# The first 512 tokens of an MLP in two halves, an attention's block means ahead of the weight loads, and a third weight matrix in the token tiles

## The chip, the cores and the metric

The kernel runs on one core of a Trainium2 chip. The metric is the time of one execution on the device in microseconds (us); the verdict compares medians of several executions. Engines are named as in the profile: PE (TensorE matmul), PEld (its weight loads), DVE (VectorE), ACT (ScalarE), POOL (GpSimd), SP (the engine that issues nearly all loads here).

## The reference

Attention over 2 batches, 8 heads, 768 positions and 64 dimensions, in which each query sees its neighbours within 16 positions and one summary per block of 32 (the maximum of the keys, the mean of the values). Its output, as 1536 tokens of 512 numbers, goes through two MLPs:

```python
def _attn_ref(q, k, v):
    k_sum = k.reshape(B, H, nb, block, D).max(axis=3)
    v_sum = v.reshape(B, H, nb, block, D).mean(axis=3)
    scores_l = np.where(mask_l, scale * q @ k.T, -1e9)          # |i - j| < 16
    scores_s = scale * einsum('bhsd,bhnd->bhsn', q, k_sum) + np.log(block)
    a = softmax(concatenate([scores_l, scores_s]))
    return a @ concatenate([v, v_sum])

x = attention as (1536, 512)
h = x @ w_in;  x = (h * sigmoid(1.702 * h)) @ w_out             # d_ff 2048, "layer 1"
x = (sigmoid(x @ w_gate) * (x @ w_val)) @ w_out2                # d_ff 1536, "layer 2"
```

The weights come in 64 bit floats.

## The kernel before

**Attention in 24 units.** A unit is one batch `b`, one group `g` of 256 query positions and one pair of heads `hp`; four units (all `hp`) make 256 tokens complete. A loop over `t` runs the parts of several units in one iteration (the list `ORDER`): scaled key windows `kx` on POOL (`w_copy`), scores `ps_s` on PE (`b_pe`: a mask matmul, then 4 of 128 columns), the row maximum `nm` on DVE, the exponential `e` on ACT (`b_exp`), the normalization on POOL, then for the unit three before it the transposes `ps_p`, their copy `pt`, the product with the value windows `ps_x` (`d_pe`), and the split of the result into two float32r tiles, `xH` on ACT and `xL` on DVE. `ps_s` has three PSUM buffers, so the mask matmul of unit u waits until the exponentials of unit u-3 are done.

**The means of the values** come from `vt`: `sum_load` brings it, `sum_v` reduces it on DVE (`vm`), `sum_lay` lays it out by PE and ACT (`ps_v`, `vs`), and `put_v` writes `vs` by DMA into the value windows `vwin`, which `d_pe` reads.

**Weights.** `fetch` loads one matrix of a group of 256 hidden columns twice, as `raw` and as a copy shifted by two bytes, `mid` (1 MB each); `load_group` decodes the pair on DVE and ACT (L104 to L119) into two float32r tiles, and each decode issues the next `fetch`. `raw` and `mid` have one buffer each; the second matrix (`1_0_1`) goes into free buffers of the token tiles `xH` and `xL`.

**MLP steps.** A step is (layer, group, block of 512 tokens). `first` makes 24 matmuls of 512 columns into `ps_h`, and the gating on ACT, DVE, ACT, POOL (`sg`, `gh`, `gl`); `second` makes 24 more into `ps_o` and adds them into `acc`. The first `EARLY` = 4 steps (blocks 0 and 1, groups 0 and 1) are put between the units of the attention by `filler`: one yield per iteration of `t`, two from t = 8, and no step before its tokens are complete (t = 10 for block 0, t = 18 for block 1). The exponential and the sigmoid use different tables of ACT, so a table is loaded at every change. The other steps follow the attention, with more PSUM buffers.

**What sets the order.** A scheduler places the instructions of PE, DVE, ACT and POOL; SP keeps the order in which the program is written. So a load that waits for a tile holds up all loads written behind it.

Of the kernel before, what the change touches and what calls it, by code (L numbers as in the profile page):

```python
# [8 lines left out]
F32 = mybir.dt.float32  # L9
F32R = mybir.dt.float32r  # L10
# [19 lines left out]
def attention_moe_moe2_kernel(ctx: ExitStack, tc: tile.TileContext, ins: dict, out: bass.AP):  # L30
    nc = tc.nc
# [92 lines left out]
    groups = [(1, g) for g in range(n1)] + [(2, g) for g in range(n2)]  # L124
    steps = [(1, g, blk) for blk in range(NTB) for g in range(2)]
    steps += [(layer, g, blk) for layer, g in groups[2:] for blk in range(NTB)]
    ends = {1: n1 - 1, 2: n2 - 1}
# [55 lines left out]

    def project(wh, wl, f, blk, name):
        ps = ps_h.tile([P, TB], F32, tag="h", name=name)
        c = slice(f * P, (f + 1) * P)
        mm3(ps, [((wh[:, kk, c], wl[:, kk, c]), (xH[blk][:, kk, :], xL[blk][:, kk, :])) for kk in range(KC)])
        return ps

    def first(layer, g, blk, batch=False):  # L190
        w = weights[layer, g]
        gh = gh_slots.tile([P, GF, TB], F32R, f"gh{layer}_{g}_{blk}")
        gl = gl_slots.tile([P, GF, TB], F32R, f"gl{layer}_{g}_{blk}")
        gt[layer, g, blk] = gh, gl

        def sigmoid(layer, ps):
            sg = sg_slots.tile([P, TB], F32, "sg")
            nc.scalar.activation(sg, ps, AF.Sigmoid, scale=1.702 if layer == 1 else 1.0)  # L198
            return sg

        def gated(f, ps, sg):
            nc.vector.tensor_tensor(out=sg, in0=ps, in1=sg, op=ALU.mult)  # L202
            nc.scalar.copy(gh[:, f, :], sg)  # L203
            nc.gpsimd.tensor_tensor(out=gl[:, f, :], in0=sg, in1=gh[:, f, :], op=ALU.subtract)  # L204

        if batch:
            held = []
            for f in range(GF):
                held.append(project(w[0], w[1], f, blk, "ps_h"))
                yield  # L210
            held = [(ps, sigmoid(layer, ps)) for ps in held]
            yield
            for f, (ps, sg) in enumerate(held):
                gated(f, ps, sg)
            yield
            return
        for f in range(GF):
            ps = project(w[0], w[1], f, blk, "ps_h")
            sg = sigmoid(layer, ps)
            if layer == 2:  # L220
                ps = project(w[2], w[3], f, blk, "ps_v")
            gated(f, ps, sg)
            yield

    def second(layer, g, blk, last, lag=False):
        w = weights[layer, g]
        wh, wl = w[-2], w[-1]
        gh, gl = gt.pop((layer, g, blk))
        if g == 0:
            acc[layer, blk] = (acc_a if blk < 2 else acc_b).tile([P, 4, 512], F32, tag=f"acc{blk}", name=f"acc{layer}_{blk}")  # L230
# [4 lines left out]
        for m in range(4):  # L235
            ps = ps_o.tile([P, 512], F32, tag=o_tag, name="ps_o")
            c = slice(m * P, (m + 1) * P)
            if layer == 1:
                mm3(ps, [((wh[:, f, c], wl[:, f, c]), (gh[:, f, :], gl[:, f, :])) for f in range(GF)])
            elif last and blk == NTB - 1 and m == 3:  # L240
# [14 lines left out]
            if g == 0:  # L255
                nc.scalar.copy(a[:, m, :], ps)
                if not lag:
                    yield
                continue
            nc.vector.tensor_tensor(out=a[:, m, :], in0=ps, in1=a[:, m, :], op=ALU.add)  # L260
            if last and layer == 1:
# [8 lines left out]
    acc_b = None  # L270
    EARLY = 4
    coming = (x for n in range(2) for x in load_group(*groups[n]))
# [10 lines left out]
    with tc.manual_schedule(engines={mybir.EngineType.SP}), ExitStack() as es:  # L283
# [225 lines left out]
        def filler():  # L509
            for layer, g, blk in steps[:EARLY]:  # L510
# [50 lines left out]
    with tc.manual_schedule(engines={mybir.EngineType.SP}):  # L561
# [66 lines left out]
```

## Time and profile before

| | |
|---|---|
| median of 3 executions | 665.69 us (665.18 to 666.26) |
| the profiled execution | 663.71 us, of which the span from first to last instruction is 661.9 |
| PE busy | 631.7 us, 95% of the span, 3168 matmuls |
| DVE, ACT, POOL busy | 415.2, 243.1, 187.2 us |
| mean granted clock of PE | 0.982 |
| moved by DMA | 93.97 MB, 142 GB/s over the span |

The span is to be read in two parts. From about 146 us to the end PE is busy without a gap, and nothing but the number and the width of its matmuls counts. Before that the attention runs with the first MLP steps between its units, and PE has gaps and stretches at half clock. The rows below show this first part.

### The profile page before, as it was taken

To read this page: it belongs to the slowest core of one execution; us is meant where nothing else is said; L and a number is where in the kernel's file an instruction comes from. 1 tells how busy PE (TensorE), PEld (TensorE's weight loads), DVE (VectorE), ACT (ScalarE), POOL (GpSimd) and SP (SyncE) were. 2 spreads that over 40 slices of the span, in tenths; PEclk is the share of its full clock that TensorE was granted. 3 is DMA by queue.
4 is the path that set the end of the run, shared out by engine and by line. 5 is a ranking of instruction groups with operands and counts; after the bars stand their busy time and mean duration, and the time that the engine had idled before them with its cause. 6 is when DMAs were issued, how large, how long until landed. Compare 5 with 4: busy or idle time off the path is not lost.

```text
span 661.9 us, 8251 instructions
## 1 busy us (share of the span) xinstructions
PE 631.7 (95%) x3168; PEld 515.1 (78%) x3170; DVE 415.2 (63%) x604; ACT 243.1 (37%) x498; POOL 187.2 (28%) x164
## 2 busy tenths in 40 slices
PE   6478799999999999999999999999999999999997
PEld 3255688778888888888888888888888888888886
DVE  6899656559998777777778626437627627422223
ACT  3355574746443333333345425313213213211110
POOL 6574576413332222213131112111111111211110
PEclk9778899999999999999999999999999999999999
DMA  9999773007775242434333034423414413000013
GB/s 314 351 372 325 223 236 94 3 13 276 255 261 198 93 171 99 159 111 145 118 138 111 20 124 143 147 92 140 176 66 151 182 49 128 0 1 0 13 67 112
DMA packets 39672, 93.97 MB, mean 142 GB/s; under 512 B 2128, under 2 KB 12624, under 8 KB 39632
## 3 DMA queue, kind: packets, MB, share of 16 engines
q1 hardware_dynamic: 39056, 92.39, 40.3%
q10 hardware_dynamic: 576, 1.05, 0.4%
q8 instruction: 25, 0.41, 0.2%
q14 instruction: 15, 0.12, 0.1%
HBM read 88.71 MB, written 3.15 MB: 139 GB/s over the span
## 4 chain that ended last, share of the span: by engine, by line
PE 88%; DVE 3%; DMA 3%; ACT 3%; POOL 1%; issue 1%; SPq 0%; DVEq 0%; ACTq 0%; POOLq 0%
PE ps_o L181 35%; PE ps_h L181 34%; PE ps_v L181 15%; DMA mid<-in_moe_w_in 2%; PE ps_s L381 2%; PE ps_x L429 1%; PE ps_p L414 1%; ACT e L394 1%; DMA vt<-in_vt 1%; DVE nm L386 1%; POOL kx L370 0%; ACT L198 0%; ACT L394 0%; DVE dc L110 0%; DVE dc L112 0%
## 5 line engine op out<-in xcount | busy, mean ns | idle before, releaser
L204 POOL TENSOR_TENSOR gl<-sg,gh 128x512 fp32r<-128x512 f32 x84 | 116.1, 1383 | 419.4 <-ACT gh L203 419.3
L260 DVE TENSOR_TENSOR acc<-ps_o,acc 128x512 f32<-128x512 f32 x143 | 96.3, 684 | 37.2 <-PE ps_o L181 36.8
L203 ACT CAST gh<-sg 128x512 fp32r<-128x512 f32 x84 | 52.1, 621 | 134.9 <-DVE sg L202 134.9
L198 ACT ACTIVATE sg<-ps_h 128x512 f32<-128x512 f32 x84 | 49.8, 596 | 139.2 <-PE ps_h L181 139.1
L202 DVE TENSOR_TENSOR sg<-ps_v,sg 128x512 f32<-128x512 f32 x36 | 24.8, 690 | 110.5 <-PE ps_v L181 110.0
L181 PE MATMUL ps_o<-gl,w_1H 128*128 128x512 f32 x192 | 75.6, 394 | 0.7 <-POOL gl L204 0.7
L181 PE MATMUL ps_o<-gh,w_1L 128*128 128x512 f32 x192 | 75.6, 400 | 0.5 <-ACT gh L203 0.4
L181 PE MATMUL ps_h<-xL,w_0H 128*128 128x512 f32 x192 | 75.7, 394 | 0.0
L181 PE MATMUL ps_h<-xH,w_0L 128*128 128x512 f32 x192 | 75.3, 396 | 0.0
L181 PE MATMUL ps_h<-xH,w_0H 128*128 128x512 f32 x192 | 75.3, 392 | 0.0
L181 PE MATMUL ps_o<-gh,w_1H 128*128 128x512 f32 x192 | 75.1, 391 | 0.0
L181 PE MATMUL ps_o<-w_2L,gh 128*128 128x512 f32 (+1 forms) x146 | 56.4, 386 | 0.0
L181 PE MATMUL ps_o<-w_2H,gl 128*128 128x512 f32 (+1 forms) x146 | 56.4, 386 | 0.0
L181 PE MATMUL ps_o<-w_2H,gh 128*128 128x512 f32 (+1 forms) x146 | 56.4, 386 | 0.0
L181 PE MATMUL ps_h<-yH,w_0L 128*128 128x512 f32 x144 | 56.0, 389 | 0.0
L181 PE MATMUL ps_h<-yL,w_0H 128*128 128x512 f32 x144 | 56.0, 389 | 0.0
L181 PE MATMUL ps_h<-yH,w_0H 128*128 128x512 f32 x144 | 56.0, 389 | 0.0
L181 PE MATMUL ps_v<-yH,w_1L 128*128 128x512 f32 x144 | 56.0, 389 | 0.0
L181 PE MATMUL ps_v<-yL,w_1H 128*128 128x512 f32 x144 | 56.0, 389 | 0.0
L181 PE MATMUL ps_v<-yH,w_1H 128*128 128x512 f32 x144 | 56.0, 389 | 0.0
L202 DVE TENSOR_TENSOR sg<-ps_h,sg 128x512 f32<-128x512 f32 x48 | 32.8, 685 | 30.1 <-ACT sg L198 30.1
L112 DVE SCALAR_TENSOR_TENSOR dc<-da,dc 128x1024 uint32<-128x1024 uint32 x34 | 48.6, 1429 | 0.5
(80 smaller groups left out, 1077.0 us busy)
## 6 DMA issues: line engine op xcount, KB each, us to landing
raw<-in_moe_w_out SPq DMA_DIRECT2D x13, 1024.0 KB, 4.9
mid<-in_moe_w_out SPq DMA_DIRECT2D x13, 1023.5 KB, 6.8
raw<-in_moe_w_in SPq DMA_DIRECT2D x8, 1024.0 KB, 5.3
mid<-in_moe_w_in SPq DMA_DIRECT2D x8, 1023.0 KB, 7.2
raw<-in_moe_w_gate SPq DMA_DIRECT2D x6, 1024.0 KB, 5.1
raw<-in_moe_w_val SPq DMA_DIRECT2D x6, 1024.0 KB, 5.0
mid<-in_moe_w_gate SPq DMA_DIRECT2D x6, 1023.0 KB, 7.1
mid<-in_moe_w_val SPq DMA_DIRECT2D x6, 1023.0 KB, 7.1
```

What stands on the lines that cost most here:

```text
L112: nc.vector.scalar_tensor_tensor(out=c, in0=a, scalar=0x80000000, in1=c, op0=ALU.bitwise_and, op1=ALU.bitwise_or)
L181: nc.tensor.matmul(ps, lhsT=a, rhs=b, start=i == 0, stop=i == n - 1)
L198: nc.scalar.activation(sg, ps, AF.Sigmoid, scale=1.702 if layer == 1 else 1.0)
L202: nc.vector.tensor_tensor(out=sg, in0=ps, in1=sg, op=ALU.mult)
L203: nc.scalar.copy(gh[:, f, :], sg)
L204: nc.gpsimd.tensor_tensor(out=gl[:, f, :], in0=sg, in1=gh[:, f, :], op=ALU.subtract)
L260: nc.vector.tensor_tensor(out=a[:, m, :], in0=ps, in1=a[:, m, :], op=ALU.add)
L381: nc.tensor.matmul(ps[:, j, :], lhsT=t[:, j, :], rhs=kt[:, j, :], start=False, stop=j == G - 1)
L386: nc.vector.tensor_reduce(out=nm, in_=live["s", u], axis=AX.X, op=ALU.max, negate=True)
L394: nc.scalar.activation(e[:, j, :], s[:, j, :], AF.Exp, bias=nm[:, j:j + 1], accum_out=sm[:, j:j + 1])
L414: nc.tensor.transpose(ps[:, j, :], e[:, j, :], ident)
L429: nc.tensor.matmul(ps[64 * e:64 * e + 64, j, :], lhsT=vw(b, g * G + j)[:, h * D:(h + 1) * D], rhs=t[:, j, 64 * e:64 * e + 64], start=True, ...
```

## The change

- The steps on block 0 are taken in halves of 256 tokens (`t0:t1`): group 0 first half, group 0 second half, group 1 first half, group 1 second half; then block 1 as before. `EARLY` is 6, so the same work stands between the units. A half may begin when its own 256 tokens are complete (t = 6 for the first), and `filler` has two yields per iteration from t = 6.
- The loads at the start are written in another order: the value sums' `vt` early, both loads of `vwin` ahead of the weights, and the two first `fetch` calls behind the `put_v` writes (which wait for `vs`). For batch 0 `vt` lies in two token tiles, so that its four loads have a place each.
- The third matrix (`1_1_0`) goes into token tiles too.
- `ps_x` has two PSUM buffers instead of one; `ps_v`, which had a bank of its own, shares them.

```diff
+    halves = [(0, 0, TB // 2), (0, TB // 2, TB)]
+    whole = [(blk, 0, TB) for blk in range(NTB)]
+    steps = [(1, g, *x) for g in range(2) for x in halves] + [(1, g, *x) for x in whole[1:] for g in range(2)]
+    steps += [(layer, g, *x) for layer, g in groups[2:] for x in whole]
...
+            homes = ((xp, "xH"), (xp, "xL")) if name in ("1_0_1", "1_1_0") else ((wraw, "raw"), (wraw, "mid"))
...
-    EARLY = 4
+    EARLY = 6
...
-        ps_t = es.enter_context(tc.tile_pool(name="ps_t", bufs=1, space=PSUM))
...
+            if b == 0:
+                if hp % 2 == 0:
+                    t = xp.tile([P, KC * TB], F32, tag="xH" if hp < 2 else "xL", name=f"vt{b}_{hp}")
+                    for i in range(2):
+                        vtl[b, hp + i] = t[:, i * S:(i + 1) * S]
...
-            ps = ps_t.tile([W0, H * D], F32, tag="t", name="ps_v")
+            ps = ps_a.tile([W0, H * D], F32, tag="x", name="ps_v", bufs=2)
...
-            ps = ps_a.tile([P, G, QB], F32, tag="x", name="ps_x")
+            ps = ps_a.tile([P, G, QB], F32, tag="x", name="ps_x", bufs=2)
...
-        load_q(0, nc.scalar)
+        for u in range(4):
+            load_q(u, nc.scalar)
         load_k(0, 0)
-        load_q(1, nc.scalar)
+        sum_load(0, 0)
         load_k(0, 1)
-        sum_load(0, 0)
-        load_q(2, nc.scalar)
+        sum_load(0, 1)
         load_k(0, 2)
-        sum_load(0, 1)
-        load_q(3, nc.scalar)
-        load_k(0, 3)
-        load_v(0, 0)
         sum_load(0, 2)
         sum_load(0, 3)
+        load_v(0, 0)
+        load_k(0, 3)
         load_q(4, nc.sync)
-        fetch()
-        fetch()
+        load_v(0, 1)
...
-                while (blk + 1) * 2 * HP - 1 + LD > now[0]:
+                layer, g, blk, _, t1 = step
+                while (blk * TB + t1) // (G * QB) * HP - 1 + LD > now[0]:
...
                 sum_lay(0)
-                load_v(0, 1)
                 put_v(0, 0)
+                fetch()
                 put_v(0, 1)
+                fetch()
...
-            for _ in range(2 if t >= 8 else 1):
+            for _ in range(2 if t >= 6 else 1):
```

Three places show how the instructions move. The first is SP, the loads around the first weights, in the kernel before (`raw`, `mid`, `xH<-in_moe_w_out` are weights, `vwin<-vs` is `put_v`):

```order
L335 DMA vt_3_148<-in_vt 128x768
L312 DMA q_150<-in_q 128x512
L153 DMA raw_0_0_152<-in_moe_w_in 128x4x512
L155 DMA mid_0_0_153<-in_moe_w_in 128x4x1023
L153 DMA xH_0_1_156<-in_moe_w_out 128x2x1024
L155 DMA xL_0_1_157<-in_moe_w_out 128x2x2047
L312 DMA q_215<-in_q 128x512
L324 DMA vwin<-in_v 96x4x512
L329 DMA vwin<-vs_219 32x4x512 x2
```

The same place after the change:

```order
L316 DMA q_145<-in_q 128x512
L328 DMA vwin<-in_v 96x4x512
L316 DMA q_203<-in_q 128x512
L333 DMA vwin<-vs_207 32x4x512
L156 DMA raw_0_0_215<-in_moe_w_in 128x4x512
L158 DMA mid_0_0_216<-in_moe_w_in 128x4x1023
L333 DMA vwin<-vs_207 32x4x512
L156 DMA xH_0_1_220<-in_moe_w_out 128x2x1024
L158 DMA xL_0_1_221<-in_moe_w_out 128x2x2047
```

The load of `vwin`, the sixth `q` and the first `put_v` now stand ahead of all weights, the second `put_v` between the two matrices.

The second place is DVE, at the row maxima of units 3 and 4 (`nm_304` and `nm_350` before) and the first instruction on the first weight matrix (`da<-raw1_0_0`), before the change:

```order
L386 TENSOR_REDUCE nm_304<-ps_s_298 128x4
L386 TENSOR_REDUCE nm_350<-ps_s_344 128x4
L341 MEMSET vm1_529 128x128
L419 COPY pt_362<-ps_p_357 128x512
L104 TENSOR_SCALAR da_258<-raw1_0_0_152 128x1024
```

After the change, with the same two row maxima named `nm_299` and `nm_345`:

```order
L459 TENSOR_TENSOR xL0_323<-ps_x_313,xH0_322 128x256
L104 TENSOR_SCALAR da_253<-raw1_0_0_215 128x1024
L395 TENSOR_REDUCE nm_299<-ps_s_293 128x4
L395 TENSOR_REDUCE nm_345<-ps_s_339 128x4
L110 TENSOR_SCALAR dc_255<-da_253 128x1024
```

The two row maxima moved from ahead of the first weight instruction to behind it.

The third place is PE where the first MLP matmuls stand. Before the change they stand among the transposes of units 7 and 8 (`ps_p_663`, `ps_p_741`), when the scores of units 0 to 11 have been made:

```order
L414 MATMUL ps_p_663<-ident_67,e_519 128x128 x4
L429 MATMUL ps_x_558<-pt_556,vwin_112 64x64 x8
L181 MATMUL ps_h_696<-xL0_328,w1_0_0H_256 128x512
L181 MATMUL ps_h_696<-xH0_327,w1_0_0H_256 128x512
L181 MATMUL ps_h_709<-xL0_328,w1_0_0H_256 128x512
L181 MATMUL ps_h_709<-xH0_327,w1_0_0H_256 128x512
L352 MATMUL ps_v_770<-ident_67,vm1_529 32x128
```

After the change, 18 matmuls of 256 columns stand ahead of the scores of unit 6 (`kx6`); the last of them is the first row here:

```order
L184 MATMUL ps_h_495<-xH0_322,w1_0_0H_251 128x256
L390 MATMUL ps_s_436<-kx6_385,q6_249 128x128 x4
L438 MATMUL ps_x_456<-pt_454,vwin_109 64x64 x8
L423 MATMUL ps_p_524<-ident_67,e_370 128x128 x4
L184 MATMUL ps_h_482<-xH0_322,w1_0_0L_252 128x256
L184 MATMUL ps_h_495<-xH0_322,w1_0_0L_252 128x256
L184 MATMUL ps_h_482<-xL0_323,w1_0_0H_251 128x256
```

The MLP begins five units earlier, in pieces of half the width. ACT has 14 table loads in its order after the change, and 8 before.

## Rows read from the trace of the kernel before

**Rows 1.** The page's 40 slices of the span, tenths: PE, clock, DMA.

```profile
PE   6478799999999999999999999999999999999997
...
PEclk9778899999999999999999999999999999999999
DMA  9999773007775242434333034423414413000013
```

**Rows 2.** Windows by stage: start:end length, busy us of each engine (instructions), clock, DMA share, GB/s.

```profile
0.00:20.00 20.00, 14.25 (x61) 8.66 (x62) 13.74 (x38) 5.81 (x25) 13.37 (x21) 1.00 0.94 327
20.00:67.00 47.00, 30.76 (x253) 22.64 (x253) 42.98 (x76) 24.91 (x90) 26.74 (x26) 0.78 1.04 347
67.00:80.00 13.00, 9.68 (x70) 6.94 (x69) 9.06 (x16) 7.11 (x17) 6.75 (x7) 0.87 0.73 195
80.00:146.00 66.00, 64.97 (x525) 52.71 (x528) 34.76 (x77) 39.84 (x129) 34.41 (x36) 1.00 0.33 96
146.00:600.00 454.00, 454.00 (x2005) 376.05 (x2004) 297.11 (x373) 157.45 (x225) 96.89 (x69) 1.00 0.36 130
```

**Rows 3.** PE's timeline: start us, busy us, instructions, in brackets idle before and releaser.

```profile
29.77 2.04 PE L381 MATMUL ps_s<-kx,q 128*128 128x128 f32 x8 [5.42 <-DMA q<-in_q]
34.01 1.12 PE L429 MATMUL ps_x<-pt,vwin 128*64 128x64 f32 x16 [2.19 <-DMA vwin<-vs]
35.98 2.05 PE L381 MATMUL ps_s<-kx,q 128*128 128x128 f32 x8 [0.85 <-DMA q<-in_q]
...
54.22 0.73 PE L181 MATMUL ps_h<-xH,w_0L 128*128 128x512 f32 x2
...
73.99 0.38 PE L379 MATMUL ps_s<-mask,pick 128*128 128x512 bf16 x1 [2.92 <-ACT e L394]
...
139.40 0.50 PE L181 MATMUL ps_o<-gl,w_1H 128*128 128x512 f32 x1 [0.66 <-POOL gl L204]
```

**Rows 4.** ACT's timeline around the first change of tables.

```profile
67.09 1.28 ACT L198 ACT_TABLE_LOAD   x1
70.04 1.09 ACT L198 ACTIVATE sg<-ps_h 128x512 f32<-128x512 f32 x2 [1.66 <-PE ps_h L181]
71.14 1.28 ACT L394 ACT_TABLE_LOAD   x1
72.44 0.37 ACT L394 ACTIVATE e<-ps_s,nm 128x128 f32<-128x128 f32 x1
```

**Rows 5.** The DMA issues: KB each, median us from issue to landing.

```profile
q<-in_q SPq DMA_DIRECT2D x20, 256.0 KB, 9.4
vwin<-in_v SPq DMA_DIRECT2D x6, 768.0 KB, 9.2
...
vwin<-vs SPq DMA_DIRECT2D x6, 256.0 KB, 8.4
```

**Rows 6.** DVE's timeline at three points of the first 67 us.

```profile
20.00 1.29 DVE L386 TENSOR_REDUCE nm<-ps_s 128x4 f32<-128x512 f32 x2 [1.12 <-PE ps_s L381]
...
21.89 0.82 DVE L104 TENSOR_SCALAR da<-raw 128x1024 f32<-128x1024 f32 x1
...
62.35 0.94 DVE L359 TENSOR_REDUCE ks<-k 128x24 f32<-128x768 f32 x1
```

**Rows 7.** PE in windows of 2 us: length, busy us, clock, DMA share, GB/s.

```profile
72.00:74.00 2.00, 0.01 (x1) 1.00 0.88 156
74.00:76.00 2.00, 1.59 (x4) 0.71 0.22 62
76.00:78.00 2.00, 2.00 (x8) 0.50 0.02 7
78.00:80.00 2.00, 2.00 (x23) 0.94 0.96 218
```

**Rows 8.** PE's timeline at the end: the first and sixth of six 256-column matmuls.

```profile
654.38 0.28 PE L181 MATMUL ps_o<-w_2H,gl 128*128 128x256 f32 x1
...
654.97 0.28 PE L181 MATMUL ps_o<-w_2H,gh 128*128 128x256 f32 x1
```

More of the change, by code (lines that the diff above doesn't have):

```diff
@@ L124, in attention_moe_moe2_kernel @@
     groups = [(1, g) for g in range(n1)] + [(2, g) for g in range(n2)]
-    steps = [(1, g, blk) for blk in range(NTB) for g in range(2)]
-    steps += [(layer, g, blk) for layer, g in groups[2:] for blk in range(NTB)]
+    halves = [(0, 0, TB // 2), (0, TB // 2, TB)]
+    whole = [(blk, 0, TB) for blk in range(NTB)]
+    steps = [(1, g, *x) for g in range(2) for x in halves] + [(1, g, *x) for x in whole[1:] for g in range(2)]
+    steps += [(layer, g, *x) for layer, g in groups[2:] for x in whole]
     ends = {1: n1 - 1, 2: n2 - 1}
@@ L182, in mm3, with project, first @@
                 i += 1
-    def project(wh, wl, f, blk, name):
-        ps = ps_h.tile([P, TB], F32, tag="h", name=name)
+    def project(wh, wl, f, blk, t, name):
+        ps = ps_h.tile([P, TB], F32, tag="h", name=name)[:, 0:t.stop - t.start]
         c = slice(f * P, (f + 1) * P)
-        mm3(ps, [((wh[:, kk, c], wl[:, kk, c]), (xH[blk][:, kk, :], xL[blk][:, kk, :])) for kk in range(KC)])
+        mm3(ps, [((wh[:, kk, c], wl[:, kk, c]), (xH[blk][:, kk, t], xL[blk][:, kk, t])) for kk in range(KC)])
         return ps
-    def first(layer, g, blk, batch=False):
+    def first(layer, g, blk, t0, t1, batch=False):
         w = weights[layer, g]
-        gh = gh_slots.tile([P, GF, TB], F32R, f"gh{layer}_{g}_{blk}")
-        gl = gl_slots.tile([P, GF, TB], F32R, f"gl{layer}_{g}_{blk}")
-        gt[layer, g, blk] = gh, gl
+        t, n = slice(t0, t1), t1 - t0
+        gh = gh_slots.tile([P, GF, TB], F32R, f"gh{layer}_{g}_{blk}_{t0}")[:, :, 0:n]
+        gl = gl_slots.tile([P, GF, TB], F32R, f"gl{layer}_{g}_{blk}_{t0}")[:, :, 0:n]
+        gt[layer, g, blk, t0] = gh, gl
         def sigmoid(layer, ps):
-            sg = sg_slots.tile([P, TB], F32, "sg")
+            sg = sg_slots.tile([P, TB], F32, "sg")[:, 0:n]
             nc.scalar.activation(sg, ps, AF.Sigmoid, scale=1.702 if layer == 1 else 1.0)
@@ L208, in first @@
             for f in range(GF):
-                held.append(project(w[0], w[1], f, blk, "ps_h"))
+                held.append(project(w[0], w[1], f, blk, t, "ps_h"))
                 yield
@@ L217, in first, with second @@
         for f in range(GF):
-            ps = project(w[0], w[1], f, blk, "ps_h")
+            ps = project(w[0], w[1], f, blk, t, "ps_h")
             sg = sigmoid(layer, ps)
             if layer == 2:
-                ps = project(w[2], w[3], f, blk, "ps_v")
+                ps = project(w[2], w[3], f, blk, t, "ps_v")
             gated(f, ps, sg)
             yield
-    def second(layer, g, blk, last, lag=False):
+    def second(layer, g, blk, t0, t1, last, lag=False):
         w = weights[layer, g]
         wh, wl = w[-2], w[-1]
-        gh, gl = gt.pop((layer, g, blk))
-        if g == 0:
+        gh, gl = gt.pop((layer, g, blk, t0))
+        if g == 0 and t0 == 0:
             acc[layer, blk] = (acc_a if blk < 2 else acc_b).tile([P, 4, 512], F32, tag=f"acc{blk}", name=f"acc{layer}_{blk}")
@@ L238, in second @@
             if layer == 1:
+                ps = ps[:, 0:t1 - t0]
                 mm3(ps, [((wh[:, f, c], wl[:, f, c]), (gh[:, f, :], gl[:, f, :])) for f in range(GF)])
@@ L255, in second @@
             if g == 0:
-                nc.scalar.copy(a[:, m, :], ps)
+                nc.scalar.copy(a[:, m, t0:t1], ps)
                 if not lag:
@@ L259, in second @@
                 continue
-            nc.vector.tensor_tensor(out=a[:, m, :], in0=ps, in1=a[:, m, :], op=ALU.add)
+            nc.vector.tensor_tensor(out=a[:, m, t0:t1], in0=ps, in1=a[:, m, t0:t1], op=ALU.add)
             if last and layer == 1:
@@ L333, in sum_load @@
         def sum_load(b, hp):
-            t = vp.tile([P, S], F32, tag="vt", bufs=2, name=f"vt{b}_{hp}")
-            nc.sync.dma_start(out=t, in_=vt[b, hp])
-            vtl[b, hp] = t
+            if b == 0:
[3 more added lines that the diff above has]
+                        vtl[b, hp + i] = t[:, i * S:(i + 1) * S]
+            else:
+                vtl[b, hp] = vp.tile([P, S], F32, tag="vt", bufs=2, name=f"vt{b}_{hp}")
+            nc.sync.dma_start(out=vtl[b, hp], in_=vt[b, hp])
         def sum_v(b, hp):
@@ L509, in filler @@
         def filler():
-            for layer, g, blk in steps[:EARLY]:
-                while (blk + 1) * 2 * HP - 1 + LD > now[0]:
+            for step in steps[:EARLY]:
+                layer, g, blk, _, t1 = step
+                while (blk * TB + t1) // (G * QB) * HP - 1 + LD > now[0]:
                     yield
                 need(layer, g, len(mats[layer]) - 1)
-                yield from first(layer, g, blk, batch=True)
+                yield from first(*step, batch=True)
                 need(layer, g, len(mats[layer]))
-                yield from second(layer, g, blk, False, True)
+                yield from second(*step, False, True)
         now = [0]
@@ L572, in attention_moe_moe2_kernel @@
         for step in steps[EARLY:]:
-            layer, g, blk = step
+            layer, g, blk = step[:3]
             need(layer, g, len(mats[layer]) - 1)
```

1 line of the change is left out of this document (removed).

## The prediction

> **What bounds the kernel now.** I read the slices first, then windows, then the timelines of single engines. The slices [rows 1] are to show where PE is not full: the first nine, some 146 us. The windows [rows 2] put numbers to it: from 146 us on PE is busy 454.0 of 454 us, 2005 matmuls at 454/2005 = 0.226 us each; PE's work there can't be shortened by this change. Ahead of 146 us it is idle 20 - 14.25 = 5.8, 47 - 30.76 = 16.2, 13 - 9.68 = 3.3 and 66 - 64.97 = 1.0 us in the four stages, 26 us in all, and it loses more at half clock (mean 0.78 from 20 to 67 us). So a gain must come from work that PE does earlier within the first 80 us.
>
> What PE waits for there changes with time. Up to about 70 us the DMA engines are full (share 0.94 and 1.04), and DVE, which decodes the weights, is busy 43.0 of 47 us from 20 to 67 [rows 2]: two bounds side by side. PE stands 5.42 us until the sixth unit's q lands at 29.77, which was issued behind 4 MB of weights, and then 2.19 us for the means in the value windows [rows 3]. The first MLP matmul runs at 54.22. The next long wait is 2.92 us at 73.99: the mask matmul of unit 15 waits for the exponentials of unit 12 [rows 3], which stand on ACT behind two table loads and two sigmoids [rows 4]. I use that point, **the gate**, to compare the two kernels: the same instruction is in both orders, and behind it the stage is PE's.
>
> **The change, part by part.** Times are set against the profiled execution, 663.71 us with a span of 661.9; the median of the runs is 665.69, and I add the same difference to it. A measurement of this kernel can tell about 0.2% from no change.
>
> *Loads.* Ahead of the first weight matrix now stand one more value window (768 KB), one more q and one put_v (256 KB each) [rows 5]: 1.3 MB, at the 347 GB/s of the stage [rows 2] 3.8 us. The units from the seventh on need q that stands behind the same bytes as before, and the keys of batch 1 (unit 12 on) as well, so with full DMA engines they land when they did. The waits of 5.42 and 2.19 us go, but what comes next is late anyway: unit 6 needs its q behind the 4 MB, as before, at about 36 us [rows 3]. I cost the gain of the reordering in itself at nothing. The third matrix's own place frees SP from a wait for the decode; with the DMA engines full that brings no byte forward, so nothing either. put_v now holds SP until the means are laid out; the loads already queued (some 1.5 MB, 4 us) cover about 15 to 19 us, so that costs nothing; without that cover it would cost the difference once, 1 to 2 us.
>
> *DVE up to the gate.* The row maxima of units 3 and 4 ran at 20.00, ahead of the first weight instruction at 21.89 [rows 6]. Now they stand behind it, and the weights land later: at the earliest when the 7.7 MB that stand up to and with that load are through (6.5 MB are moved by 20 us, 20 x 327 GB/s [rows 2], the rest at 347: 23.4), at the latest 21.89 + 3.8 = 25.7. I take 24.4, the middle, since neither end has a nearer row. DVE is then 2.5 us later at that instruction and has 0.9 us of work less behind it than it had there (its order up to that point, form by form): 3.4 us behind. Up to the key maxima of batch 1, which ran at 62.35 [rows 6], its order holds 1.1 us more (two half gate products, some sums). I expect these maxima at 62.35 + 3.4 + 1.1 = 66.9, ended at 67.8. Behind them follow: xL of unit 7 (0.4), the last six half matmuls (0.7), two half sigmoids (0.55, half of the 1.09 in [rows 4]), a gate product, a cast and xH (about 0.4 each), a table load of 1.28 and four exponentials (1.45, four of 0.36): the gate opens at 67.8 + 0.4 + 0.7 + 0.55 + 1.2 + 1.28 + 1.45 = 73.4, against 73.99. Term: -0.6 us, between -2 (weights at 23.4 and DVE's waits of before gone) and +2 (weights at 25.7 and new waits on top).
>
> *What PE has done at the gate.* By the order, 24 MLP matmuls of 512 columns stand ahead of it before, and 84 of 256, worth 42, after. 18 x 0.226 = 4.1 us that need not be done later; one group of transposes (0.45) has gone to the other side. Term: **-3.6 us**, counted from the order and a measured spacing, the surest one.
>
> *Clock.* Behind its idle time PE ran at 0.71, 0.50 and 0.94 [rows 7]: 1.59 x 0.29 + 2 x 0.5 + 2 x 0.06 = 1.6 us lost. After the change PE has 12 half matmuls and a unit's products just ahead of the gate and stands there for about 1 us. I take the whole 1.6 as gained; the other end is 0, if the thinner work of 57 to 67 us drops the clock instead.
>
> *Width.* 256 columns take (654.97 - 654.38)/5 = 0.118 us [rows 8], against 0.113 for half of 0.226. 192 of them cost 22.7 where 96 cost 21.7: **+0.9 us**, all on PE.
>
> *Tables.* The order holds six table loads more, 6 x 1.28 = 7.7 us on ACT, which has time for them (39.8 of 66 us busy [rows 2]) but not always slack: three PSUM buffers of scores tie PE to exponentials three units back. Before, seven loads fall between 67 and 146 us, and PE's waits that end with that chain are 2.92 and 0.66 [rows 3], with 0.2 in small pieces 3.8 us: 0.54 per load. Six more at that price: +3.3 us. The ends are 0 (all covered) and 7.7 (all exposed).
>
> The Trainium skill ("ScalarE: Activation LUTs", Rules for kernel authors) says to group functions by table set and to budget about 2.7 us per switch, 1.28 of it the load and the rest a drain. The trace agrees with the 1.28 and shows no drain behind the load: the exponential starts at 72.44, 0.02 us after the load of 71.14 ends [rows 4]. By the page the six switches would take 16 us of ACT rather than 7.7, which is an estimate and enters nothing here.
>
> *Buffers.* The second ps_x buffer removes waits on xL, which lie in the DMA-bound part: 0. ps_v in that place holds one of the two buffers for a few us around units 9 and 10, with the means of batch 1: 0, and 1 us if the next ps_x meets it.
>
> **Sum:** -0.6 - 3.6 - 1.6 + 0.9 + 3.3 = -1.6 us: 662.1 for the profiled execution, 665.69 - 1.6 = **664.1** for the median.
>
> **The rivals.**
>
> *Tables decide (slower).* After the gate the filler gives each unit only half the matmuls that it had (6 worth 512 columns an iteration until block 0 is done). Where an exponential waits behind a switch, PE has 12 half matmuls, 1.4 us, to bridge 1.28 + 1.45 and a sigmoid. Places: units 13, 17 and 22, and the last early step, where PE has one product of 0.6 us left beside its own chain. If all six loads are exposed, the term is 7.7 rather than 3.3: -1.6 + 4.4 = +2.8, 668.5. It decides from 0.8 us per load on. For it: the 2.92 us at 73.99. Against it: from 80 to 146 us PE lost 1.0 us with five loads [rows 2]. Chance 0.23.
>
> *DVE is later (no change).* If the weights land at the late end, 25.7, or the decode meets new waits, the gate opens 1 to 2 us later and eats the rest: about 665.6. For it: DVE has only 4 us of slack between 20 and 67. Chance 0.22. That the first half can't start early, so that the change doesn't do what it says, ends here too.
>
> *Everything is covered (faster).* The gate 1.4 earlier than I have it and no new load exposed: -1.6 - 1.4 - 3.3 = -6.3, 659.4. For it: nearly all waits between 80 and 146 us were covered before. Against: there is less to cover with. Chance 0.20.
>
> The Trainium skill's rule on table sets (same page) speaks for the first rival; its own price would put it at some 8 us more than mine, an estimate that the 0.02 us above speaks against.
>
> **How the numbers follow.** The forecast, within 1.5 us of 664.1, has 0.35. Of it some 0.6 lies below 0.2% (1.3 us): faster 0.21 + 0.20, and 0.02 from the edges of the others, is 0.43. Same: 0.14 of the forecast and 0.16 of the DVE case, 0.30. Slower: 0.23 and 0.04 from a later gate, 0.27. The range runs from 659.5, the covered case, to 669.0, a little beyond the exposed one.
>
> **What would show it.** The gate (mask matmul of unit 15, [rows 3]) near 73.4 with 84 half matmuls done. The first weight instruction on DVE at 24 to 25 us, the row maxima of units 3 and 4 behind it. The first MLP matmul near 33 to 35 us rather than 54. DMA still full to about 70 us. Half matmuls 0.118 apart. PE's clock whole from 74 to 80 us. Idle of PE between 80 and 146 us: 3 to 5 us, ended by exponentials or gl. It is wrong if the key maxima of batch 1 stay at 62 us (then faster), if that idle exceeds 7 us (slower), or if PE is still in gaps up to 146 us.

## The result, and the profile after

The changed kernel takes 670.18 us in the median (668.89 to 670.93), the kernel before beside it 665.57: a ratio of 1.0076, 95% interval [1.0057, 1.0095]. It is 4.6 us slower; the prediction had 664.1 us, 1.6 faster, and its range ended at 669.0. The two profiled executions lie further apart than the medians, 669.2 and 661.9 us of span.

The slices of the changed kernel (PE, clock, DMA), which answer to [rows 1]:

```profile
PE   7577899789999999999999999999999999999997
...
PEclk9779799999999999999999999999999999999999
DMA  9998684007853343434342233333423423000013
```

Its windows, with the columns of [rows 2]:

```profile
0.00:20.00 20.00, 13.96 (x50) 8.11 (x50) 13.42 (x39) 6.26 (x26) 11.62 (x19) 1.00 0.95 308
20.00:67.00 47.00, 33.23 (x301) 29.23 (x302) 38.08 (x68) 27.02 (x90) 29.41 (x27) 0.85 0.98 316
67.00:80.00 13.00, 10.03 (x69) 8.43 (x67) 12.13 (x21) 9.28 (x28) 8.04 (x7) 0.74 0.89 303
80.00:146.00 66.00, 59.27 (x565) 50.32 (x563) 33.11 (x81) 43.05 (x134) 34.30 (x39) 1.00 0.34 103
146.00:600.00 454.00, 452.52 (x1993) 373.80 (x1994) 298.87 (x378) 157.84 (x225) 96.78 (x70) 1.00 0.36 130
```

PE is busier up to 67 us (33.2 of 47 us rather than 30.8, at a clock of 0.85 rather than 0.78), as the change wants it. Behind 80 us it is idle 66 - 59.27 = 6.7 us, where the kernel before lost 1.0, and it still has gaps behind 146 us, 1.5 us.

A measure that holds both gaps and half clock is length less busy time times clock. Two windows show the parts (PE busy, clock, DMA share, GB/s). The kernel before:

```profile
0.00:80.00 80.00, 54.69 (x381) 0.85 0.96 317
80.00:170.00 90.00, 88.97 (x631) 1.00 0.44 141
```

The changed kernel:

```profile
0.00:80.00 80.00, 57.23 (x418) 0.87 0.96 312
80.00:170.00 90.00, 81.78 (x661) 1.00 0.42 133
```

Lost from 80 to 170 us: 90 - 88.97 = 1.0 us before, 8.2 after. Up to 80 us the whole window gives 80 - 54.69 x 0.85 = 33.5 us before and 30.2 after, but its clock is a mean that holds PE's idle time too. Summed over windows of 1 us it is 32.6 before and 31.1 after. So 1.5 us are gained and 7.2 lost again; with the prediction's 0.9 us for the narrow matmuls that makes 6.6 of the 7.3 us between the two spans. I use this pair of numbers, from windows of 1 us, for all kernels below.

Where the 8.2 us go stands in PE's timeline of the changed kernel (start, busy, idle before and releaser). It also has the wait for the means, the first MLP matmul, and at 78.24 the gate:

```profile
24.05 1.33 PE L438 MATMUL ps_x<-pt,vwin 128*64 128x64 f32 x20 [2.53 <-DMA vwin<-vs]
...
37.99 0.56 PE L184 MATMUL ps_h<-xH,w_0L 128*128 128x256 f32 x1
...
78.24 0.38 PE L388 MATMUL ps_s<-mask,pick 128*128 128x512 bf16 x1 [1.59 <-ACT e L403]
...
90.45 0.38 PE L388 MATMUL ps_s<-mask,pick 128*128 128x512 bf16 x1 [1.25 <-ACT e L403]
...
106.31 0.38 PE L388 MATMUL ps_s<-mask,pick 128*128 128x512 bf16 x1 [1.06 <-ACT e L403]
...
128.91 0.50 PE L184 MATMUL ps_o<-gh,w_1L 128*128 128x512 f32 x1 [2.29 <-DVE sg L206]
...
133.78 0.69 PE L438 MATMUL ps_x<-pt,vwin 128*64 128x64 f32 x16 [1.30 <-DVE pt L428]
```

ACT ahead of the longest of these waits:

```profile
123.42 1.28 ACT L403 ACT_TABLE_LOAD   x1 [1.16 <-DVE nm L395]
...
126.24 1.28 ACT L202 ACT_TABLE_LOAD   x1
127.53 0.60 ACT L202 ACTIVATE sg<-ps_h 128x512 f32<-128x512 f32 x1
...
129.53 1.28 ACT L403 ACT_TABLE_LOAD   x1
```

Three loads in 7.4 us, in the fifth of the six early steps: the sigmoid that PE waits for at 128.91 stands behind the exponentials of one unit and two of these loads, and the next unit's exponentials behind the third; their sums hold DVE, and with it the copy `pt` that PE waits for at 133.78.

### The profile page after: what moved, and what is told of

Its sections match the earlier page's. It is cut to its first block, busy times and chain, and to the rows that moved or that the text cites. A ratio compares the mean times of both kernels' runs of the same rounds, so it can differ in the third digit from the quotient of the medians.

```text
span 669.2 us, 8465 instructions
## 1 busy us (share of the span) xinstructions
PE 634.3 (95%) x3266; PEld 524.0 (78%) x3266; DVE 414.6 (62%) x612; ACT 252.6 (38%) x516; POOL 190.5 (28%) x168
## 3 DMA queue, kind: packets, MB, share of 16 engines
q10 hardware_dynamic: 576, 1.05, 0.4%
## 4 chain that ended last, share of the span: by engine, by line
PE 84%; ACT 5%; DVE 5%; DMA 3%; issue 1%; POOL 1%; SPq 0%; DVEq 0%; ACTq 0%; POOLq 0%
PE ps_h L184 33%; PE ps_o L184 33%; PE ps_v L184 15%; ACT e L403 2%; DMA mid<-in_moe_w_in 2%; PE ps_s L390 2%; ACT L403 1%; ACT L202 1%; DMA k<-in_k 1%; PE ps_x L438 1%; PE ps_p L423 1%; DVE nm L395 1%; DVE db L108 1%; DVE sg L206 1%; ACT sg L202 0%
## 5 line engine op out<-in xcount | busy, mean ns | idle before, releaser
L208 POOL TENSOR_TENSOR gl<-sg,gh 128x512 fp32r<-128x512 f32 (+1 forms) x88 | 117.1, 1332 | 425.9 <-ACT gh L207 415.4
L265 DVE TENSOR_TENSOR acc<-ps_o,acc 128x512 f32<-128x512 f32 (+1 forms) x147 | 97.2, 670 | 37.0 <-PE ps_o L184 36.5
L202 ACT ACTIVATE sg<-ps_h 128x512 f32<-128x512 f32 (+1 forms) x88 | 50.5, 577 | 141.5 <-PE ps_h L184 141.3
L207 ACT CAST gh<-sg 128x512 fp32r<-128x512 f32 (+1 forms) x88 | 52.7, 602 | 133.3 <-DVE sg L206 133.3
L184 PE MATMUL ps_o<-gh,w_1L 128*128 128x512 f32 (+1 forms) x208 | 77.2, 379 | 3.0 <-DVE sg L206 2.3
L184 PE MATMUL ps_h<-xL,w_0H 128*128 128x512 f32 (+1 forms) x208 | 79.0, 380 | 0.8 <-DVE xL L459 0.7
L184 PE MATMUL ps_h<-xH,w_0L 128*128 128x512 f32 (+1 forms) x208 | 79.4, 384 | 0.0
L184 PE MATMUL ps_o<-gl,w_1H 128*128 128x512 f32 (+1 forms) x208 | 78.2, 377 | 1.2 <-POOL gl L208 1.2
L184 PE MATMUL ps_h<-xH,w_0H 128*128 128x512 f32 (+1 forms) x208 | 78.6, 378 | 0.0
L184 PE MATMUL ps_o<-gh,w_1H 128*128 128x512 f32 (+1 forms) x208 | 77.5, 374 | 0.0
L206 DVE TENSOR_TENSOR sg<-ps_h,sg 128x512 f32<-128x512 f32 (+1 forms) x52 | 33.4, 645 | 33.3 <-ACT sg L202 33.2
```

Source lines behind the costliest of these rows:

```text
L184: nc.tensor.matmul(ps, lhsT=a, rhs=b, start=i == 0, stop=i == n - 1)
L265: nc.vector.tensor_tensor(out=a[:, m, t0:t1], in0=ps, in1=a[:, m, t0:t1], op=ALU.add)
```

## The experiments

Each kernel was timed in five rounds beside the kernel before on the same chip. In e3 and e8 PE's matmuls stand in the order of the changed kernel, in e4 and e7 in that of the kernel before, in e9 and e11 in that of e5, in e14 in that of e9 and in e18 in that of e2 (by the traces up to 190 us). In the others the scheduler rewrites PE's order with the edit, so the price of a part is that of the part and of the order that comes with it; the number of table loads changes too and stands in the table below.

**Halves alone, loads alone (e1, e2).** e1 is the kernel before with the new steps, its loads, tiles and PSUM pools untouched:

```diff
-    steps = [(1, g, blk) for blk in range(NTB) for g in range(2)]
+    steps = [(1, g, *x) for g in range(2) for x in halves] + [(1, g, *x) for x in whole[1:] for g in range(2)]
...
-    EARLY = 4
+    EARLY = 6
...
-            for _ in range(2 if t >= 8 else 1):
+            for _ in range(2 if t >= 6 else 1):
```

e2 is the changed kernel with whole first tokens:

```diff
-    halves = [(0, 0, TB // 2), (0, TB // 2, TB)]
+    halves = [(0, 0, TB)]
...
-    EARLY = 6
+    EARLY = 4
...
-            for _ in range(2 if t >= 6 else 1):
+            for _ in range(2 if t >= 8 else 1):
```

> The changed kernel with the loads of the kernel before: the same six early steps with four halves, but the order of the first loads, the home of the third matrix, the tiles of the value sums and the PSUM pools are those of before. Theory L (the late weights are the cause: DVE's first weight instruction at 26.5 us instead of 21.9 shifts the gate from 74.0 to 78.2): the weights are early again, the gate comes at 73 to 74 us, and the kernel is at 664 to 666 us, 4 to 6 us under the changed one. Theory T (the halves themselves: table switches and thin work between units after the gate): the waits of PE from 80 to 170 us stay at 6 to 8 us, and the time is 668 to 671.

> The changed kernel with the first 512 tokens taken whole again (four early steps, the filler at its old rate): only the loads, the tiles and the PSUM buffers are new. Theory L: the weights are as late as in the changed kernel (first weight instruction on DVE at 26 us or later), the gate comes 3 to 5 us later than before, and the time is 668 to 671. Theory T: the loads cost nothing by themselves, 664 to 667, and PE's waits from 80 to 170 us are near the 1 us of before.

Measured: e1 675.28 us, ratio 1.0161 [1.0143, 1.0178]; e2 668.55 us, 1.0054 [1.0037, 1.0071]. Both parts cost time, the halves 10.7 us and the rest 4.0, and together they cost 4.6. Both theories had part of it, and neither has the sum; e1 is slower than either allowed.

**Table loads (e3, e4).** One line in the changed kernel and in the kernel before; a plain copy stands where the sigmoid was, so the early steps leave the sigmoid out:

```diff
-            nc.scalar.activation(sg, ps, AF.Sigmoid, scale=...)
+            nc.scalar.activation(sg, ps, AF.Copy if batch else AF.Sigmoid, scale=...)
```

> The changed kernel with the sigmoids of the early steps replaced by plain copies of the same shape (so the MLP's first part is computed without its gate): the order on PE and DVE is the same, on ACT only twelve table loads of 1.28 us go. Theory T: the waits of PE after 80 us that end with an exponential (3.8 us of them on the path) shrink to under 2, the gate comes 1 to 2 us earlier, and the time falls by 5 to 7 us to 663 to 665. Theory L: most loads are hidden, the time falls by 1 to 2.5 us only, to 668 to 669.

> The same replacement in the kernel before: the order on PE and DVE is unchanged, on ACT six table loads go. It gives the price of a table load there. Prediction's price of 0.54 us per load: the wait of 2.92 us at the gate falls by about 2.6, and the time falls by 3 to 4 us to 662 to 663. If the loads are hidden behind something that is late as well: less than 1.5 us.

Measured: e3 662.55 us, 0.9964 [0.9951, 0.9977]; e4 661.67 us, 0.9958 [0.9943, 0.9973]. Against the changed kernel's 1.0076 that is 7.4 us for twelve loads (0.6 each); in the kernel before 2.8 us for six (0.5 each). The wait at the gate of the kernel before falls from 2.92 to 1.48 us only, so about half of it isn't the loads'. With the same PE order, PE behind 80 us in e3 (PE busy, clock, DMA share, GB/s):

```profile
80.00:146.00 66.00, 63.52 (x566) 1.00 0.40 117
146.00:170.00 24.00, 23.97 (x105) 1.00 0.75 266
```

PE is idle 2.5 us here, where the changed kernel had 8.2. The table loads are most of what is lost behind 80 us: shown. Without loads in either, the change is worth nothing (0.9964 against 0.9958).

**Means ahead of weights (e5, e6).** In e2 and in the changed kernel the first two matrices go back ahead of the second value window and the means:

```diff
         load_q(4, nc.sync)
-        load_v(0, 1)
+        fetch()
+        fetch()
...
+                load_v(0, 1)
                 put_v(0, 0)
-                fetch()
                 put_v(0, 1)
-                fetch()
```

> The kernel of e2 (whole first tokens, new loads, tiles and PSUM buffers) with the first two weight matrices issued ahead of the second value window and the means again, as in the kernel before. If the order means ahead of weights is what costs e2 its 4 us: the first weight instruction on DVE comes at about 22 us rather than 26, the key maxima of batch 1 at 62 to 63 us, and the time is 664 to 666. If it is the tiles (third matrix and value sums in token tiles) or the PSUM buffers: the time stays at 667.5 to 669.5.

> The changed kernel with the same two matrices issued ahead of the second value window and the means. If late weights are all that the order does, the decode is 4 to 6 us earlier and the time falls by 3 to 5 us to 665 to 667. If the halves need the means early (the first half's tokens are finished only when units 0 to 7 have their products), the time goes towards that of e1: 672 to 676.

Measured: e5 661.00 us, 0.9939 [0.9920, 0.9958]; e6 668.93 us, 1.0064 [1.0044, 1.0083]. With whole tokens the order of the loads is worth 7.6 us (1.0054 to 0.9939; the order of e5 also has ten table loads where that of e2 has twelve); with halves it can't be told from nothing (1.0076 to 1.0064). e5 came out below both of its forecasts, e6 between its two. And e5, which is the change without the halves and without the means' new place, is 4 us faster than the kernel before.

**Where the 4 us of e5 come from (e11, e12, e16).** e11 puts the third matrix back into `raw` and `mid`; e12 takes the PSUM pools of before; e16 is the kernel before with the PSUM part alone:

```diff
-        ps_t = es.enter_context(tc.tile_pool(name="ps_t", bufs=1, space=PSUM))
...
-            ps = ps_t.tile([W0, H * D], F32, tag="t", name="ps_v")
+            ps = ps_a.tile([W0, H * D], F32, tag="x", name="ps_v", bufs=2)
...
-            ps = ps_a.tile([P, G, QB], F32, tag="x", name="ps_x")
+            ps = ps_a.tile([P, G, QB], F32, tag="x", name="ps_x", bufs=2)
```

> The kernel of e5 with the third matrix in its old place (it waits there for the decode of the first). PE's order is the same. If the new home brings nothing because the DMA engines are full, as the prediction has it: 660 to 662, as e5. If it is the source of e5's gain: 663.5 to 665.

> The kernel of e5 with the PSUM pools of before (one ps_x buffer, one for the transposes of the means). If the second ps_x buffer brings nothing, as the prediction has it: 660 to 662. If it is the source of e5's gain (the units need not wait for xL on DVE, which is full up to 67 us): 663.5 to 666.

> The kernel before with one part of the change alone: two ps_x buffers, one of which the means' transposes use too. If that is what gives e5 its gain over e12: 660 to 662. If it needs the new order of the first loads beside it: 663.5 to 665.

Measured: e11 660.09 us, 0.9934 [0.9921, 0.9947], as e5; e12 664.88, 1.0012 [0.9998, 1.0025]; e16 660.96, 0.9942 [0.9925, 0.9958]. The second `ps_x` buffer, with the order that comes with it, is the gain, 3.8 us by itself. The matmuls into `ps_x` alone in two windows (16 for each unit) show its way; the kernel before:

```profile
0.00:57.00 57.00, 4.30 (x80) 0.85 1.01 335
57.00:80.00 23.00, 3.86 (x80) 0.85 0.86 274
```

and e16:

```profile
0.00:57.00 57.00, 5.55 (x112) 0.85 1.01 335
57.00:80.00 23.00, 3.35 (x72) 0.93 0.83 267
```

By 57 us seven units have their products rather than five, and at the gate (73.62 us; 73.99 before) 32 MLP matmuls are done rather than 24. With one buffer a product can't begin until DVE has taken `xL` of the unit before, and `xL` stands among the decodes on a DVE that is full there [rows 2]. That this is the way of the gain is argued: the trace of the kernel before puts only 0.9 us of waits in front of `ps_x` down to `xL`, and the order of PE changed with the buffer.

**Sigmoids without a table load (e7, e8).** A sigmoid can be written with a hyperbolic tangent, sigmoid(x) = (1 + tanh(x / 2)) / 2, and e7 and e8 do so in the early steps:

```diff
-            nc.scalar.activation(sg, ps, AF.Sigmoid, scale=1.702 if layer == 1 else 1.0)
+            nc.scalar.activation(sg, ps, AF.Tanh if batch else AF.Sigmoid, scale=0.851 if batch else ...)
...
+                nc.vector.scalar_tensor_tensor(out=sg, in0=sg, scalar=1.0, in1=ps, op0=ALU.add, op1=ALU.mult)
...
-                nc.scalar.copy(a[:, m, t0:t1], ps)
+                nc.scalar.activation(a[:, m, t0:t1], ps, AF.Copy, scale=0.5 if lag else 1.0)
...
+            if lag:
+                nc.vector.scalar_tensor_tensor(out=a[:, m, t0:t1], in0=ps, scalar=0.5, in1=a[:, m, t0:t1], op0=ALU.mult, op1=ALU.add)
```

> The kernel before with its early sigmoids written as a hyperbolic tangent (half scale in, one scalar_tensor_tensor for (t + 1) * h, a factor 0.5 where the sums leave PSUM). The Trainium skill (ScalarE: Activation LUTs, the list of table sets) names tanh in the set of exp. So the early steps need no table load, as in e4, with the right result: 661 to 663 us. If the factor 0.5 or the scalar_tensor_tensor costs ACT or DVE more than the loads gave: 664 or more.

> The changed kernel with the same hyperbolic tangent in its six early steps. Twelve loads go as in e3: 661.5 to 664 us if the loads are the price of the halves. It then tells, beside e7, what the change is worth when tables cost nothing: by e3 and e4 it is 1 us slower than e7, not faster.

Measured: e7 661.95 us, 0.9956 [0.9939, 0.9973]; e8 661.87 us, 0.9954 [0.9937, 0.9971]. ACT's table loads in e8, by line (count, busy us, mean ns, idle time before and what ended it):

```profile
L410 ACT ACT_TABLE_LOAD x1 | 1.3, 1283 | 2.7 <-issue 2.7
L202 ACT ACT_TABLE_LOAD x1 | 1.3, 1283 | 2.7 <-PE ps_h L184 2.7
```

The same in the changed kernel:

```profile
L403 ACT ACT_TABLE_LOAD x7 | 9.0, 1283 | 5.5 <-issue 2.9 <-DVE nm L395 1.4 <-DVE db L108 1.1
L202 ACT ACT_TABLE_LOAD x7 | 9.0, 1283 | 3.4 <-PE ps_h L184 3.3
```

The trace agrees with what the Trainium skill ("ScalarE: Activation LUTs", Table sets: the hidden batching unit) says of tanh: it stands in the set of exp, and between the two there is no load.

**The gains together (e9, e10).** e9 is e5 with tanh, e10 is e6 with tanh.

> The kernel of e5 (whole first tokens, weights ahead of means, new tiles and PSUM buffers) with the hyperbolic tangent of e7. If the two gains add (3.45 us of e5, 2.5 us of e7): 658 to 660 us, below every kernel so far. If what the six loads cost was already hidden in e5's order: 660 to 661.5.

> The same with the first 512 tokens in halves (e6 with the hyperbolic tangent). If the halves cost only their table loads, it is level with e9 or below it, 657 to 660, since PE can start on the first half earlier. If the halves have a price of their own (192 matmuls of 256 columns 0.9 us dearer, the thin filler between units): 1 to 4 us above e9.

Measured: e9 656.68 us, 0.9883 [0.9870, 0.9896], the fastest, 8 us under the kernel before; e10 659.63 us, 0.9922 [0.9910, 0.9935]. So the halves cost 2.6 us without any table load. PE in e10 (start, busy, idle before and releaser):

```profile
133.74 0.50 PE L184 MATMUL ps_o<-gl,w_1H 128*128 128x512 f32 x1 [1.05 <-POOL gl L211]
...
137.15 0.50 PE L184 MATMUL ps_o<-gl,w_1H 128*128 128x512 f32 x1 [0.85 <-POOL gl L211]
```

Attention has ended at 126 us, with 144 of the 192 early matmuls done, and the last early step stands alone with its own chain through ACT and POOL. A half step takes as many turns of the filler as a whole one.

**The rate of the filler (e15).** e10 with a third turn:

```diff
-            for _ in range(2 if t >= 6 else 1):
+            for _ in range(3 if t >= 6 else 1):
```

> The kernel of e10 (halves, weights first, tanh) with three turns of the filler an iteration from the seventh on, not two. If the rate is the halves' price (the last step stands alone when attention ends, with 2.9 us of waits at 120 to 146 us): those waits go, and the time comes to that of e9 plus 0.9 us for the width, 657 to 658. If the halves' own waits decide: 659 to 661.

Measured: 657.51 us (654.73 to 661.09), 0.9893 [0.9863, 0.9923]. The middle is as the rate theory has it, but the interval touches e10's, so it is likely, not shown. Halves in their best form are level with whole tokens, not ahead.

**The last keys of batch 1 (e13, e14, e17).** In the changed kernel, in e9 and in e2 the keys go ahead of the value window and the means of the same iteration:

```diff
+            if 8 <= t < 8 + HP:
+                load_k(1, t - 8)
             if t % HP == HP - 1 and HP < t < NU - HP:
                 c = t // HP + 1
                 load_v(c // NG, c % NG)
                 put_v(c // NG, c % NG)
-            if 8 <= t < 8 + HP:
-                load_k(1, t - 8)
```

> The changed kernel with the last keys of batch 1 issued ahead of the value window and the means that hold them back. If they are what turns the early work into a loss: their maxima run at 80 to 82 us rather than 88.8, and the time falls by 3 to 6 us to 663 to 666. If the table loads and the late weights do it by themselves: under 1.5 us, 668 to 670.

> The kernel of e9 (weights first, whole tokens, tanh) with the same keys ahead. PE waits there for nothing from 80 us on, so the keys are covered by MLP work: 656 to 657, no change. If they hold attention back so that its end is later: 1 to 3 us under e9.

> The kernel of e2 (whole first tokens, means ahead of weights, sigmoids as they are) with the last keys of batch 1 issued ahead of the means of that batch. If the late keys make PE's waits at 93 to 105 us: their maxima come at 81 us rather than 85.2, and the time falls by 4 to 7 us to 661 to 664. If not: 667 to 669.

Measured: e13 670.18 us, 1.0072 [1.0050, 1.0094]; e14 656.93, 0.9882 [0.9861, 0.9903]; e17 662.27, 0.9967 [0.9954, 0.9980]. In e13 the last key maxima run at 80.05 us rather than 88.84, and nothing is gained in the median; in its trace, which is that of its fastest execution (667.42 us), the waits behind 80 us lie between 100 and 150 us. In e2 the same step gives 5.8 us. In both the order of PE changes with the step and two table loads go (twelve for fourteen in e13, ten for twelve in e17), so the 5.8 us are not those of the keys alone.

**e2 without table loads (e18).**

> The kernel of e2 with the hyperbolic tangent in its early steps, so without its six table loads. If the means-first order costs through the table loads (four of them stand between the late keys and PE's waits): 657 to 660, near e9. If it costs as much without them: 664 to 665, 4.3 us (what e9 gained on e5) under e2.

Measured: 658.05 us, 0.9903 [0.9885, 0.9921], 10 us under e2. (e2 has twelve table loads in its order, not eight as the kernel before, so ten go and not six.) So e2's price is the meeting of two things: the keys come late and then four table loads stand between them and PE. Either remedy takes most of it away, and without the loads the means-first order costs 1.3 us (0.9883 to 0.9903), which is not clear of noise: the two intervals overlap. DVE in e2 at the last keys (start, busy, idle before and releaser):

```profile
85.21 0.95 DVE L368 TENSOR_REDUCE ks<-k 128x24 f32<-128x768 f32 x1 [3.45 <-DMA k<-in_k]
```

ACT in e2 behind them:

```profile
86.88 0.37 ACT L403 ACTIVATE e<-ps_s,nm 128x128 f32<-128x128 f32 x1 [5.44 <-DVE nm L395]
...
88.67 1.28 ACT L202 ACT_TABLE_LOAD   x1
...
90.57 1.28 ACT L403 ACT_TABLE_LOAD   x1
...
93.39 1.28 ACT L202 ACT_TABLE_LOAD   x1
...
96.76 1.28 ACT L403 ACT_TABLE_LOAD   x1
```

ACT stands 5.44 us while PE uses up its MLP matmuls, and then loads tables for 5.1 of 9.4 us while PE has only two left there.

The whole in one table: the table loads in ACT's order, and the lost time of PE worked out as above from windows of 1 us:

| kernel | ratio to before | table loads | lost to 80 us | lost 80 to 170 us |
|---|---|---|---|---|
| before | 1 | 8 | 32.6 | 1.0 |
| e1: before, halves | 1.0161 | 12 | 31.9 | 10.2 |
| e12: weights first, whole, one `ps_x` | 1.0012 | 8 | 33.1 | 1.2 |
| e16: before, two `ps_x` | 0.9942 | 10 | 29.2 | 2.5 |
| e5: weights first, whole | 0.9939 | 10 | 28.9 | 2.8 |
| e2: means first, whole | 1.0054 | 12 | 27.9 | 9.2 |
| e6: weights first, halves | 1.0064 | 14 | 26.8 | 11.2 |
| changed kernel: means first, halves | 1.0076 | 14 | 31.1 | 8.2 |
| e8: changed kernel, tanh | 0.9954 | 2 | 28.7 | 2.3 |
| e18: e2, tanh | 0.9903 | 2 | 28.2 | 0.1 |
| e9: e5, tanh | 0.9883 | 2 | 27.2 | 0.1 |
| e10: e6, tanh | 0.9922 | 2 | 23.3 | 4.2 |

Every kernel of the table with a second `ps_x` buffer gains 1.5 to 9.3 us up to 80 us, and the two others without it at most 0.7. What tells them apart is what they pay behind it: 8 to 11 us with twelve or fourteen table loads, 1 to 3 with eight or ten, 0 to 4 with two.

## Why the prediction was wrong

**What bounds the kernel** was read rightly: up to 80 us the loads and DVE, behind 146 us PE alone. In the prediction's own terms two steps failed and one was mis-sized. The gain booked at the gate (-0.6 and -3.6 us) failed, since the gate came 4.25 us later and not 0.6 earlier: the loads were priced too fast, and the chain behind the key maxima took 8.7 us rather than 5.6. The second `ps_x` buffer at nothing failed (-3.8 us in e16). The tables were mis-sized: +3.3 us, where the runs have 4.6 to 5.2, and behind the gate PE was idle for 6.7 us up to 146, where 3 to 5 were expected.

The likeliest case was the wrong one. The rival "tables decide", with 668.5 us and 0.23, came nearest, and its mechanism is what happened: PE waits behind table loads (e3, e8). That its number is so near is luck. It has all six further loads exposed, 7.7 us, where they cost 4.6 to 5.2, and it keeps -4.9 us for everything else, where the runs have -0.1. The places that it names are right: PE waits 1.25 us behind the exponentials of unit 13 (at 90.45), 1.06 behind those of unit 17 (at 106.31), 2.29 behind those of unit 22 and the sigmoid after them (at 128.91), and 1.75 in all in the last early step (146 to 151 us).

**Loads: the step failed.** It took the stage's mean of 347 GB/s for 1.3 MB. A value window, a q and the first of the two writes of means stand there, and they move slower at the same full share. The changed kernel (DVE busy, clock, DMA share, GB/s) while they pass, and then with weights:

```profile
18.00:20.00 2.00, 0.97 (x4) 1.00 1.06 246
20.00:22.00 2.00, 0.00 (x0) 1.00 1.08 256
22.00:24.00 2.00, 0.00 (x0) 0.62 1.04 225
24.00:26.00 2.00, 0.38 (x1) 0.50 1.06 388
```

At some 240 GB/s the 1.3 MB take 5.4 us, not 3.8. That the DMA engines stay full to 70 us was wrong too: from 58 to 62 us SP stood behind a wait, and their share was 0.46 and 0.13 in the two windows of 2 us. But early weights alone don't mend the change: in e6 the first weight instruction comes at 20.97 us, the key maxima at 64.92 and the gate at 77.14 with 48 matmuls' worth done, and the time is the same; PE loses 11.2 us behind 80 us there.

**DVE up to the gate: mis-sized by 4.9 us.** DVE in the changed kernel:

```profile
25.62 0.42 DVE L459 TENSOR_TENSOR xL<-ps_x,xH 128x256 fp32r<-128x256 f32 x1 [6.32 <-ACT xH L456]
26.47 0.69 DVE L104 TENSOR_SCALAR da<-raw 128x1024 f32<-128x1024 f32 x1 [0.42 <-DMA raw<-in_moe_w_in]
...
68.62 0.94 DVE L368 TENSOR_REDUCE ks<-k 128x24 f32<-128x768 f32 x1
```

The first weight instruction comes at 26.47 us, not 24.4 (21.89 before), and DVE stands idle for 6.3 us ahead of it. The key maxima come at 68.62, not 66.9, and the gate opens at 78.24, not 73.4: +4.25 us against before where the term had -0.6. Of these 4.9 us 1.7 stand at the key maxima. The chain behind them took 8.7 us and not 5.6: ACT has a decode instruction of 1.05 us there that the sum leaves out, and stands 0.79 and 1.09 us:

```profile
70.77 0.81 ACT L202 ACTIVATE sg<-ps_h 128x256 f32<-128x256 f32 x2 [0.30 <-PE ps_h L184]
71.48 1.05 ACT L105 ACTIVATE da<-da 128x1024 f32<-128x1024 f32 x1
...
73.92 0.37 ACT L456 CAST xH<-ps_x 128x256 fp32r<-128x256 f32 x1 [0.79 <-PE ps_x L438]
75.38 1.28 ACT L403 ACT_TABLE_LOAD   x1 [1.09 <-DVE db L108]
```

Without table loads the changed kernel has the gate at 75.97 us (e8), the kernel before at 74.72 (e7), so most of the delay goes with the loads and 1.25 us are left. The gate in e8:

```profile
75.97 0.38 PE L395 MATMUL ps_s<-mask,pick 128*128 128x512 bf16 x1 [0.30 <-ACT e L410]
```

**PE's MLP work at the gate: counted right, and no gain.** 42 matmuls' worth are done there, as forecast, but 4.25 us later, and 18 x 0.226 is 4.1 us: a wash. The first of them runs at 37.99 us, not at 33 to 35. The prediction called this its surest term. A count at an instruction is a gain only if the instruction comes when it is expected.

**Clock.** From 74 to 80 us the clock is whole, as forecast; half clock has moved to 66 to 73 us, so little of the 1.6 us was gained.

**Width** was right as far as the trace goes: the matmuls of 256 columns follow each other at 0.12 us where PE isn't held up and the clock is whole (from 82.71 to 84.50 us).

**Tables: mechanism right, 1 to 2 us too small.** The price of a load, 0.54 us from the trace of before, agrees with 0.5 (e4) and 0.6 (e3), in part by luck: it took the whole 2.92 us at the gate for the loads', and 1.48 of them stay without any (e4). The six more loads cost 7.4 - 2.8 = 4.6 us by copies and 8.1 - 2.9 = 5.2 by tanh, where the sum had 3.3. Why a load costs more in one order than in another isn't shown: eight loads cost e5 3.7 us (e5 to e9, 0.5 each), ten cost e2 10 us (e2 to e18, 1.0 each). That the early MLP matmuls which had covered the loads were already gone fits PE's waits, but no run changes that cover alone.

**Buffers: the step failed.** The second `ps_x` buffer was costed at 0, since its waits lie in the DMA-bound part; e16 has -3.8 us. That part is bound by DVE as well, and with the buffer the products come earlier there. No run takes the buffer out of the changed kernel; that its gain stands in it and is outweighed is assumed.

**The sum again, without table loads** (e7, e18, e9, e10, e8): `ps_x` and the other loads -4.8 us (e7 to e9), means first +1.3 (e9 to e18), halves +3.4 (e18 to e8): -0.1 us, where the prediction had -4.9. With the tables' 5.2 that is +5.1, against 4.6 to 5.0 measured. These are differences along one chain of kernels, so they add up by their making, and the agreement is no check of its own; +1.3 is within the noise of its two runs. What stays open is how the 3.4 us of the halves split into the filler's rate, the width and the chain of the last step.

## What to carry to other kernels

Work that is pulled forward is taken from a place where it may have covered something: cost that place anew before booking the gain, since here 1.5 us were won up to 80 us and 7.2 lost behind. Run the parts of a change singly: the buffer beside the named parts gave 3.8 us by itself, and the whole change shows nothing of it. Where two functions on ACT alternate, first ask whether one of them can be written with a function of the other's set; that was worth 2.9 us in the kernel before and 8 in the changed one. And price a transfer at its own rate, not at its stage's.

## What the hardware showed that was not expected

Loads of the same DMA share differ much in speed: in e5 the weights ran at 386 to 410 GB/s from 18 to 28 us, and a q, a value window and the two writes of means at 266, 242 and 198 GB/s from 28 to 34 us, both at shares of 1.02 to 1.08. One window of each (DVE busy, clock, DMA share, GB/s):

```profile
22.00:24.00 2.00, 1.92 (x2) 1.00 1.04 410
...
32.00:34.00 2.00, 2.00 (x3) 0.50 1.08 198
```

tanh next to exp took no table load (two loads of 1.28 us in the whole of e8, fourteen in the changed kernel), while every change between exp and the sigmoid took one.
